# Fewer, wider weight transfers and an undivided filter band at the start of a convolution and maxout kernel

## The chip, the core and the metric

The kernel runs on one core of a Trainium2 chip. The metric is the device time of one execution in microseconds (us), as the median of several runs. One core has five engines with instruction streams of their own: TensorE (PE, with its weight loads shown as PEld), VectorE (DVE), ScalarE (ACT), GpSimd (POOL) and SyncE (SP), which issues nearly all transfers. Each engine takes its instructions in the order in which the program lists them, and waits for what they need.

## The reference

The input `x` is 8 sequences of 4160 tokens with 192 channels. First comes a causal convolution over 7 tokens whose weights are the softmax of a small table; the 192 channels are 8 heads of 24, and a head shares its 7 weights. Then a maxout layer with three weight matrices and an output matrix:

```python
w = softmax(weight, axis=-1)                       # 8 heads x 7 taps
out[b, s, head, c] = sum_k w[head, k] * x_pad[b, s + k, head, c]
x = out.reshape(33280, 192)
h = maximum(maximum(x @ w1, x @ w2), x @ w3)       # w1, w2, w3: 192 x 768
return h @ w_out                                   # w_out: 768 x 192
```

All of it is given and returned in 32-bit floats.

## The kernel before, in words

The 33280 tokens are 65 blocks of 512. The maximum is rewritten so that TensorE forms only two of the three products: with the differences `wd1 = w1 - w3` and `wd2 = w2 - w3`, the maximum of the three is `max(relu(y @ wd1), y @ wd2) + y @ w3`. The first part is `h`, in six column tiles `j` of 128. The rest, `y @ w3`, needs no maximum, so `w3 @ w_out` is worked out once (`m16`, by `make_m`) and is added in the output product. So the weights must land as 32-bit numbers, be subtracted (`make_wd`) and so be turned into the 16-bit `wd` before the first hidden tile can be formed.

**Steady state.** From block 2 on, each block has its hidden products (`l1`, line 521), per tile one relu on ACT (line 508) and one maximum on DVE (line 509), and the output products of the block before it (`st2`, line 585). TensorE's list is written out by hand in that order. It is without gaps from some 30 us on.

**Start.** All that the change touches lies in the first 20 us. The list of each engine there follows the order of the program text:

- Lines 241 to 245 issue, on SP: block 0's `x` (two transfers), block 1's `x` (one), then of `w3`, `w1`, `w2` the upper 128 rows in columns 0 to 255 (`load_wa`, lines 227 to 229, three transfers), the lower 64 rows of `w3` in all 768 columns (line 244, one), and the lower 64 rows of `w1` and `w2` in columns 0 to 255 (`load_wb`, lines 231 to 233, two). Behind the band's code, lines 303 to 306 issue the rest: `load_wa` for columns 256 to 511, `load_wb` for columns 256 to 767, `load_wa` for columns 512 to 767, then `w_out`, then blocks 2 and 3.
- The convolution is a product with a banded matrix `band` (128 rows, 8 heads, 134 columns). TensorE makes its 38 nonzero columns for 32 rows in two PSUM tiles (line 291, columns 0 to 27 and 28 to 37), and line 299 copies these to the four diagonal places `a` of 32 rows, ACT the wide part and DVE the narrow one, first for heads 5 to 7 and then for heads 0 to 4: 8 copies on each engine.
- `cast_dense(t, ...)` (lines 207 to 218) turns block t's `x` into 16 bits in two halves, `v` = 0 on DVE and `v` = 1 on POOL, in three column slots. For block 0 slots 1 and 2 come ahead of the band's copies and slot 0 between the two groups of heads.
- `conv_dense(t, copies, order)` (lines 384 to 401) is block t's convolution: two PSUM tiles `n`, 40 products each. `n` = 1 needs heads 5 to 7 alone, `n` = 0 needs heads 0 to 5. `copies[n]` is the engine that takes tile `n` out to `yd` (line 401).
- `copy_w3` (line 324, on ACT) copies `w3`'s lower 64 rows to the other half of the partitions, in 32 bits. `make_wd(n, j0, j1)` (line 320) makes the differences for tiles j0 to j1: `n` = 0 is `w1` upper, `n` = 1 is `w2` upper, `n` = 2 holds the lower rows of both and needs `copy_w3` for its columns.
- `l1_dense` (line 544) forms hidden tiles of blocks 0 and 1 in two parts: "F" with the upper rows (`n` = 0 and 1) and "H" with the lower ones (`n` = 2). `tops` gives for each tile one relu on ACT and one maximum on DVE (lines 508 and 509).
- `cross_wd`, `cast_w3`, `transpose_w3`, `make_m`, `first_hidden` and the casts of blocks 2 and 3 follow, and need all weights.

In what follows, "the relus 0 and 1" are those of block 0, tiles 0 and 1; then come block 1's for the same tiles, a 1.47 us fill with zeros (`zero_x(6)`, line 140, on ACT), and the relus of tiles 2 and 3.

Of the kernel before, what the change touches and what calls it, by code (L numbers as in the profile page):

```python
# [15 lines left out]
P = 128  # L16
KW = 7
PAD = KW - 1
NHEAD = 8
# [5 lines left out]
WIN = 32 + PAD  # L25
# [3 lines left out]
def kernel(  # L29
# [12 lines left out]
    nc = tc.nc  # L42
# [3 lines left out]
    H, KWs = weight.shape  # L46
    assert H == NHEAD and KWs == KW and D == GRP * NHEAD
    DFF = moe_w1.shape[1]
# [9 lines left out]
    for b in range(B):  # L58
        s = nfull * NBLK
        while s < SEQ:  # L60
            n = min(SEQ - s, NBLK - off)
# [57 lines left out]
    xin, xbuf, XBUF, loaded = {}, [], 7, set()  # L119
# [82 lines left out]
    NC, NSLOT, CYC = D // HALF, D // 32, 96  # L202
# [1 line left out]
    xz = {t: [const.tile([P, NQ, D], FP16, name=f"xz_{t}_{v}") for v in range(2)] for t in range(2)}  # L204
    xz[2], xz[3] = xz[0], xz[1]

    def cast_dense(t, copies, slots_=range(CYC // 32), keep=False):
        xf, _, parts = xin[t] if keep else xin.pop(t)
        for v, copy in enumerate(copies):
            if copy is None:  # L210
                continue
            for s in slots_:
                cut = GRP * (32 * s // GRP + 1)
                a, b = (32 * s, cut) if v == 0 else (cut, 32 * s + 32)
                for (rl, q0, q1) in parts:
                    copy(  # L216
                        out=xz[t][v][0:rl, q0:q1, :].rearrange("p q (k c) -> p q k c", c=CYC)[:, :, :, a:b],
                        in_=xf[0:rl, q0:q1, :].rearrange("p q (k c) -> p q k c", c=CYC)[:, :, :, a:b])
# [6 lines left out]
    PW = 2 * P  # L225

    def load_wa(f):
        for st, n, wsrc in ((w3s, 0, moe_w3), (ws, 0, moe_w1), (ws, 1, moe_w2)):
            nc.sync.dma_start(out=st[:, n, f], in_=wsrc[0:P, f])  # L229

    def load_wb(f):
        for st, lo, n, wsrc in ((ws, 0, 2, moe_w1), (ws, HALF, 2, moe_w2)):
            nc.sync.dma_start(out=st[lo:lo + HALF, n, f], in_=wsrc[P:D, f])
# [22 lines left out]
    def keep_warm(widths, pool, tag):  # L256

        ps = pool.tile([P, NBLK], FP32, tag=tag, name="idle")
        for n in widths:
            nc.tensor.matmul(ps[:, 0:n], lhsT=idle[:, 0:P], rhs=idle[:, 0:n], start=True, stop=True)  # L260
# [15 lines left out]
    band = bands[:, 0:NHEAD * BAND_W].rearrange("p (h w) -> p h w", w=BAND_W)  # L276
# [4 lines left out]
    nc.vector.reciprocal(out=wrec[:], in_=wrec[:])  # L281
    zero_x(4)
    nc.vector.tensor_scalar_mul(out=line[0:NHEAD, 31:31 + KW], in0=wexp[:, 0:KW], scalar1=wrec[:])
    cast_dense(0, (nc.vector.tensor_copy, nc.gpsimd.tensor_copy), (1, 2), keep=True)
    CUT = 28
    bands_ = []
    for lo, hi, copy in ((0, CUT, nc.scalar.copy), (CUT, WIN, nc.vector.tensor_copy)):
        bps = psq.tile([32, hi - lo + 3, NHEAD], FP32, tag="q", name=f"band_{lo}")
# [4 lines left out]
                             rhs=ident16[:, 0:4 * NHEAD], start=True, stop=True)  # L293
        bands_.append((lo, hi, copy, bps))
    keep_warm((NBLK, NBLK, P), psp, "p")
    for h0, h1 in ((5, NHEAD), (0, 5)):
        for lo, hi, copy, bps in bands_:
            for a in range(4):
                copy(out=band[32 * a:32 * a + 32, h0:h1, 32 * a + lo:32 * a + hi],
                     in_=bps[:, 0:hi - lo, h0:h1].rearrange("p c h -> p h c"))  # L300
        if h0:
            cast_dense(0, (nc.vector.tensor_copy, nc.gpsimd.tensor_copy), (0,))
    load_wa(slice(PW, 2 * PW))
    load_wb(slice(PW, DFF))
    load_wa(slice(2 * PW, DFF))
    nc.sync.dma_start(out=wos[:], in_=moe_w_out.rearrange("(j p) c -> p j c", p=P))
    load_x(2)
    load_x(3)
# [9 lines left out]
    def make_wd(n, j0, j1, eng=nc.vector):  # L318
        f = slice(P * j0, P * j1)
        eng.tensor_sub(out=wd[:, n, f], in0=ws[:, n, f], in1=w3s[:, n // 2, f])  # L320

    def copy_w3(copy, j0, j1):
        f = slice(P * j0, P * j1)
        copy(out=w3s[HALF:P, 1, f], in_=w3s[0:HALF, 1, f])  # L324
# [12 lines left out]
    def w_of(i, c, j):  # L337
        n = side(i, c)
        n = i if n == 0 else NC if n == 1 else 2
        return wd[HALF * i:HALF * (i + 1), n, P * j:P * (j + 1)]  # L340
# [43 lines left out]
    def conv_dense(t, copies, pools=((None, None),) * 2, order=(0, 1)):  # L384


        yd = dense[t] = ydp.tile([P, NC, NBLK], FP16, tag="yd", name=f"yd_{t}")
        for n in order:
            slots_ = ((0, 1, 2, 3), (4, 5, 4, 5))[n]
            pool, tag = pools[n]  # L390
            ps = (pool or psw).tile([P, NBLK], FP32, tag=tag or "w", name=f"D{n}_{t}")
            for (q, b, row_lo, rlen, lo, hi, cc) in chunks_of[t]:
                for v in range(2):
                    for g, s in enumerate(slots_):
                        h = (32 * s + 31 * v) // GRP
                        nc.tensor.matmul(  # L396
                            ps[32 * g:32 * g + 32, lo:hi],
                            lhsT=xz[t][v][0:rlen, q, 32 * s:32 * s + 32],
                            rhs=band[0:rlen, h, cc:cc + hi - lo],
                            start=(v == 0), stop=(v == 1), tile_position=(0, 32 * g))  # L400
            copies[n](out=yd[:, 2 * n, :], in_=ps[:])
# [49 lines left out]
    def y_all(t, i, c):  # L451
        if t < NDENSE:
            return dense[t][HALF * i:HALF * (i + 1), side(i, c), :]
        a = y_row(t, i)
        s0, s1, s2, s3 = (spot(t, i, c, r) for r in range(4))
        assert s3 - s2 == s1 - s0
        return bass.AP(tensor=a.tensor, offset=a.offset + P * s0,
                       ap=[list(a.ap[0]), [P * (s2 - s0), 2], [P * (s1 - s0), 2], [1, P]])
# [39 lines left out]
    def meet():  # L498

        emit(True)  # L500
        assert not ops
        clock[0] = clock[1] = 0

    def top(t, j, ps):
        if t not in hs:
            hs[t] = hp.tile([P, NJ, NBLK], FP16, tag="h", name=f"h_{t}")
        r = rp.tile([P, NBLK], FP16, tag="r", name=f"r_{t}_{j}")
        nc.scalar.activation(out=r[:], in_=ps[0][:], func=AF.Relu)  # L508
        nc.vector.tensor_max(out=hs[t][:, j, :], in0=r[:], in1=ps[1][:])  # L509
        done[t] = j + 1  # L510
# [20 lines left out]
    def l1_dense(tiles, parts="FH"):  # L531

        meet()
        for n, part in enumerate(parts):
            for t, j, pools in tiles:
                for i, (pool, tag) in enumerate(pools):
                    if (t, j, i) not in open_ps:
                        open_ps[t, j, i] = pool.tile([P, NBLK], FP32, tag=tag, name=f"l{tag}{i}_{t}_{j}")
                        begun.discard((t, j, i))
                    if part == "F":  # L540
                        a, b = wd[:, i, P * j:P * (j + 1)], dense[t][:, 0, :]
                    else:
                        a, b = w_of(i, NC - 1, j), y_all(t, i, NC - 1)
                    nc.tensor.matmul(open_ps[t, j, i][:], lhsT=a, rhs=b,  # L544
                                     start=(t, j, i) not in begun, stop=(t, j, i) in begun)
                    begun.add((t, j, i))

    def tops(*tiles):
        for t, j in tiles:
            top(t, j, (open_ps[t, j, 0], open_ps[t, j, 1]))  # L550
# [139 lines left out]
    PQ = ((psp, "p"), (psq, "q"))  # L690
    WW = ((psw, "w"), (psw, "w"))
    WPWQ = ((psw, "w"), (psp, "p"), (psw, "w"), (psq, "q"))
    ACT, DVE = nc.scalar.copy, nc.vector.tensor_copy
    GP = nc.gpsimd.tensor_copy
    conv_dense(0, (ACT, ACT), order=(1, 0))
    cast_dense(1, (DVE, GP), (1, 2, 0))
    zero_x(5, eng=nc.gpsimd)
    make_wd(0, 0, 2)
    make_wd(1, 0, 2)
    copy_w3(ACT, 0, 2)  # L700
    make_wd(2, 0, 2)
    conv_dense(1, (DVE, ACT), order=(1, 0))
    copy_w3(ACT, 2, 6)
    for n in range(NC):
        make_wd(n, 2, 4, nc.gpsimd)
    for n in range(NC):
        make_wd(n, 4, 6, nc.gpsimd)
    cast_w3(0, 6)
    GP(out=wo[:], in_=wos[:])
    l1_dense([(0, 0, PQ), (0, 1, PQ)], "F")  # L710
    l1_dense([(0, 0, PQ), (0, 1, PQ)], "H")
    tops((0, 0), (0, 1))
    l1_dense([(1, 0, WW), (1, 1, WW)], "HF")
    tops((1, 0), (1, 1))
    zero_x(6)
# [135 lines left out]
```

## Time and profile before

| | before |
|---|---|
| median of 3 runs | 453.19 us (453.03 to 454.11) |
| profiled execution, its own time | 454.16 us |
| its span, first to last instruction | 452.4 us |
| TensorE busy | 445.5 us, 98% of the span |
| mean granted TensorE clock | 1.000 of full speed |
| first gapless hidden products of block 2 (line 521) begin | 24.4 us |
| transfers of `w1`, `w2`, `w3` | 14 issues of 64 to 192 KB, by lines 229, 233 and 244 |

Times in the profile's rows are in us from the start of the span. A row of the timeline has start, duration, engine, line, operation, output and inputs, and how many instructions it merges; in brackets stands how long the engine had been idle and what released it. With `x2` the duration is that of both together. The chain of work that ended last is followed back from the last instruction. A row of the windows has, for one stretch, its length, the busy time of PE, PEld, DVE, ACT and POOL, the clock granted to TensorE, the busy share of the 16 DMA engines and the GB/s.

### The profile page before, as it was taken

What the parts mean: (1) busy time and instruction counts of PE and PEld (TensorE: products, weight loads), DVE (VectorE), ACT (ScalarE), POOL (GpSimd) and SP (SyncE); (2) the same over time, 40 slices, a digit from 0 to 9 for tenths busy, and PEclk for the clock granted to TensorE, in tenths of its full rate; (3) what the DMA queues carried; (4) which work ended last, traced back from release to release, by engine and by line L of the source; (5) the groups of instructions that cost most, each with busy time, mean ns of one, the idle gap of its engine ahead of it and who ended that gap; (6) DMA issues with size and microseconds to landing.
All of it is one profiled execution on the core that took longest, in us unless ns stands there. A gap on an engine that the chain in (4) does not pass through costs nothing.

```text
span 452.4 us, 18264 instructions
## 1 busy us (share of the span) xinstructions
PE 445.5 (98%) x7576; PEld 409.8 (91%) x7576; DVE 354.6 (78%) x607; ACT 320.2 (71%) x601; POOL 207.6 (46%) x239
## 2 busy tenths in 40 slices
PE   7999999999999999999999999999999999999997
PEld 4469999999999989999999999999999999999996
DVE  6668787878878787787887787887887887887775
ACT  6967767767777677676676776777776776776664
POOL 5864836556463533724824635525533644224000
PEclk9999999999999999999999999999999999999999
DMA  7968987696885659649649748657649668152123
GB/s 197 239 181 167 203 186 197 155 217 171 170 220 147 165 137 205 162 121 199 167 127 198 178 110 191 191 114 193 178 112 197 172 157 143 54 136 75 58 71 106
DMA packets 128163, 72.01 MB, mean 159 GB/s; under 512 B 52305, under 2 KB 127888, under 8 KB 128080
## 3 DMA queue, kind: packets, MB, share of 16 engines
q1 hardware_dynamic: 127919, 70.75, 65.9%
q8 instruction: 59, 0.97, 0.9%
q14 instruction: 25, 0.20, 0.2%
q10 hardware_dynamic: 160, 0.10, 0.1%
HBM read 33.28 MB, written 25.56 MB: 130 GB/s over the span
## 4 chain that ended last, share of the span: by engine, by line
PE 96%; DMA 1%; ACT 1%; SPq 1%; issue 1%; DVE 0%; ACTq 0%
PE po L585 36%; PE lq L521 32%; PE lp L521 22%; PE G L375 3%; DMA wall<-in_moe_w_dram 1%; ACT r L508 1%; PE D L396 1%; PE po L643 0%; PE po L616 0%; PE lw L544 0%; SPq L229 0%; SPq L167 0%; PE pm L355 0%; ACT wall L324 0%; PE lq L544 0%
## 5 line engine op out<-in xcount | busy, mean ns | idle before, releaser
L585 PE MATMUL po<-wo,h 64*128 64x192 f16 x3024 | 331.7, 243 | 0.0
L509 DVE TENSOR_TENSOR h<-r,lq 128x512 f16<-128x512 f16 x384 | 263.0, 686 | 86.2 <-ACT r L508 76.3
L508 ACT ACTIVATE r<-lp 128x512 f16<-128x512 f32 x384 | 228.9, 597 | 113.8 <-PE lp L521 103.0
L521 PE MATMUL lp<-yp,wd 64*128 64x512 f16 x1098 | 295.6, 376 | 0.0
L521 PE MATMUL lq<-yp,wd 64*128 64x512 f16 x1098 | 295.5, 376 | 0.0
L585 PEld LDWEIGHTS <-h 64*128 64x128 f16 x3024 | 242.7, 94 | 5.4 <-issue 4.1
L521 PEld LDWEIGHTS <-wd 64*128 64x128 f16 x2268 | 181.7, 94 | 14.8 <-issue 0.2
L199 POOL CAST x<-xf 103x768 f16<-103x768 f32 x122 | 97.3, 825 | 114.4 <-DMA xf<-in_x_dram 99.6
L585 PE MATMUL po<-m,yp 64*128 64x192 f16 x720 | 140.3, 243 | 0.0
L438 POOL COPY yp<-yp 64x1536 f16<-64x1536 f16 (+1 forms) x70 | 90.9, 1298 | 86.0 <-DMA yp<-ys 49.1
L593 DVE TENSOR_TENSOR o<-a,po 128x384 f32<-128x384 f32 x126 | 69.0, 547 | 0.0
L585 PEld LDWEIGHTS <-yp 64*128 64x128 f16 x720 | 66.3, 94 | 0.1
L592 ACT COPY a<-po 128x384 f32<-128x384 f32 x126 | 59.6, 473 | 0.0
L415 ACT CAST ys<-G 128x480 f16<-128x480 f32 (+1 forms) x53 | 25.4, 530 | 9.5 <-PE G L375 9.2
L415 DVE CAST ys<-G 128x480 f16<-128x480 f32 (+1 forms) x53 | 30.1, 610 | 0.0
L375 PE MATMUL G<-x,band 39*32 39x240 f16 (+3 forms) x1024 | 16.5, 242 | 0.0
L375 PEld LDWEIGHTS <-band 39*32 39x32 f16 x1024 | 10.2, 92 | 4.6 <-issue 4.1
L521 PE MATMUL lq<-yd,wd 64*128 64x512 f16 x36 | 9.7, 376 | 0.0
L521 PE MATMUL lp<-yd,wd 64*128 64x512 f16 x36 | 9.7, 376 | 0.0
L544 PEld LDWEIGHTS <-wd 128*128 128x128 f16 (+1 forms) x48 | 3.0, 95 | 7.3 <-issue 1.7
L396 PEld LDWEIGHTS <-xz 112*32 112x32 f16 x320 | 4.1, 96 | 2.9 <-issue 1.4
L216 POOL CAST xz<-xf 112x160 f16<-112x160 f32 (+2 forms) x18 | 5.1, 328 | 3.2 <-DMA xf<-in_x_dram 3.0
(75 smaller groups left out, 100.0 us busy)
## 6 DMA issues: line engine op xcount, KB each, us to landing
xf<-in_x_dram SPq DMA_DIRECT2D x113, 234.0 KB
out_dram<-o SPq DMA_DIRECT2D x62, 384.0 KB
xf<-in_x_dram SPq DMA_DIRECT2D x7, 204.8 KB
wall<-in_moe_w_dram SPq DMA_DIRECT2D x11, 128.0 KB
xf<-in_x_dram SPq DMA_DIRECT2D x3, 420.0 KB
yp<-ys SPq DMA_TRANSPOSE x70
out_dram<-o SPq DMA_DIRECT2D x5, 192.0 KB
wos<-in_moe_w_out_dram SPq DMA_DIRECT2D x1, 576.0 KB
```

What stands on the lines that cost most here:

```text
L199: nc.gpsimd.tensor_copy(out=x16s[t0][0:K, :, :, u, r, :].rearrange("p h j c -> p j h c"), in_=xf[0:K, 4 * r:4 * r + 4, :].rearrange("p j ( ...
L216: copy(out=xz[t][v][0:rl, q0:q1, :].rearrange("p q (k c) -> p q k c", c=CYC)[:, :, :, a:b], in_=xf[0:rl, q0:q1, :].rearrange("p q (k c) -> ...
L375: nc.tensor.matmul(G[2 * (k // per) + i][TOK * j:TOK * (j + 1), k % per, :], lhsT=band[row, h, HALF * i + LAP:HALF * i + KR], rhs=x16s[t0] ...
L396: nc.tensor.matmul(ps[32 * g:32 * g + 32, lo:hi], lhsT=xz[t][v][0:rlen, q, 32 * s:32 * s + 32], rhs=band[0:rlen, h, cc:cc + hi - lo], star ...
L415: copy(out=slots[t][:, i % 2, :, :, GRP * h0:GRP * (h0 + per)].rearrange("p u r (h c) -> p h (u r) c", c=GRP), in_=G[i][:].rearrange("p h ...
L438: nc.gpsimd.tensor_copy(out=yp[HALF * i:HALF * (i + 1), 1, :, :, :, :].rearrange("p i u k n -> p (i u k n)"), in_=yp[HALF * (1 - i):HALF * ...
L508: nc.scalar.activation(out=r[:], in_=ps[0][:], func=AF.Relu)
L509: nc.vector.tensor_max(out=hs[t][:, j, :], in0=r[:], in1=ps[1][:])
L521: nc.tensor.matmul(ps[i][:], lhsT=w_of(i, c, j), rhs=y_all(t, i, c), start=(n == 0), stop=(n == NC - 1))
L585: nc.tensor.matmul(ps[b0, i][:, s % 2, :], lhsT=a, rhs=b, start=first, stop=last)
L592: nc.scalar.copy(out=a[:], in_=ps[s - 1, 0][:])
L593: nc.vector.tensor_add(out=outs[t][:, s - 1:s + 1, :], in0=a[:], in1=ps[s - 1, 1][:])
```

## The change

Four things are altered, all in the first part of the program:

1. The band is copied for all heads at once and for three of the four places; the fourth place is copied by POOL from the first (16-bit, from on-chip memory). Block 0's casts are no longer split around it, and block 0's convolution takes `n` = 0 first.
2. The upper rows of the weights come in two column pieces (256 and 512 columns) and no longer in three, so the second `load_wa` covers columns 256 to 767 and stands ahead of the second `load_wb`: three issues fewer. The transfer of `w3`'s lower 64 rows, whole already, is as before.
3. Block 1's convolution tile `n` = 0 is taken out by ACT and no longer by DVE.
4. `copy_w3` for tiles 2 to 5 stands behind the relus of tiles 0 and 1 in ACT's list. POOL's list of `make_wd` is in the same order as before, with the text around it moved.

```diff
-    def cast_dense(t, copies, slots_=range(CYC // 32), keep=False):
-        xf, _, parts = xin[t] if keep else xin.pop(t)
+    def cast_dense(t, copies, slots_=range(CYC // 32)):
+        xf, _, parts = xin.pop(t)
...
-    cast_dense(0, (nc.vector.tensor_copy, nc.gpsimd.tensor_copy), (1, 2), keep=True)
+    cast_dense(0, (nc.vector.tensor_copy, nc.gpsimd.tensor_copy))
...
-    for h0, h1 in ((5, NHEAD), (0, 5)):
-        for lo, hi, copy, bps in bands_:
-            for a in range(4):
-                copy(out=band[32 * a:32 * a + 32, h0:h1, 32 * a + lo:32 * a + hi],
-                     in_=bps[:, 0:hi - lo, h0:h1].rearrange("p c h -> p h c"))
-        if h0:
-            cast_dense(0, (nc.vector.tensor_copy, nc.gpsimd.tensor_copy), (0,))
-    load_wa(slice(PW, 2 * PW))
+    for lo, hi, copy, bps in bands_:
+        for a in range(3):
+            copy(out=band[32 * a:32 * a + 32, :, 32 * a + lo:32 * a + hi],
+                 in_=bps[:, 0:hi - lo, :].rearrange("p c h -> p h c"))
+    nc.gpsimd.tensor_copy(out=band[96:P, :, 96:96 + WIN], in_=band[0:32, :, 0:WIN])
+    load_wa(slice(PW, DFF))
     load_wb(slice(PW, DFF))
-    load_wa(slice(2 * PW, DFF))
...
-    conv_dense(0, (ACT, ACT), order=(1, 0))
+    conv_dense(0, (ACT, ACT))
...
-    conv_dense(1, (DVE, ACT), order=(1, 0))
+    conv_dense(1, (ACT, ACT), order=(1, 0))
+    make_wd(0, 2, 4, nc.gpsimd)
+    make_wd(1, 2, 4, nc.gpsimd)
+    l1_dense([(0, 0, PQ), (0, 1, PQ)], "F")
+    l1_dense([(0, 0, PQ), (0, 1, PQ)], "H")
+    tops((0, 0), (0, 1))
     copy_w3(ACT, 2, 6)
-    for n in range(NC):
-        make_wd(n, 2, 4, nc.gpsimd)
+    make_wd(2, 2, 4, nc.gpsimd)
     for n in range(NC):
         make_wd(n, 4, 6, nc.gpsimd)
     cast_w3(0, 6)
     GP(out=wo[:], in_=wos[:])
-    l1_dense([(0, 0, PQ), (0, 1, PQ)], "F")
-    l1_dense([(0, 0, PQ), (0, 1, PQ)], "H")
-    tops((0, 0), (0, 1))
     l1_dense([(1, 0, WW), (1, 1, WW)], "HF")
```

## The prediction

> **What bounds the kernel now.** I read the page first.
>
> ```profile
> PE 445.5 (98%) x7576; PEld 409.8 (91%) x7576; DVE 354.6 (78%) x607; ACT 320.2 (71%) x601; POOL 207.6 (46%) x239
> ```
>
> TensorE is the bound over the span, so the change, which takes no product away, can only move the time at which TensorE comes to its gapless work. I therefore read the chain that ended last for the first 30 us.
>
> ```profile
> 3.71 6.13 DMA wall<-in_moe_w_dram
> 9.86 0.40 ACT wall L324
> 10.29 0.58 ACT yd L401
> 10.90 0.62 ACT wall L324
> ...
> 15.12 0.61 ACT r L508
> 15.75 0.70 DVE h L509
> ...
> 16.49 0.38 PE lq L544
> ```
>
> The chain starts from a transfer (`w3`'s lower 64 rows, landing at 9.84), runs along ACT's own list to 15.73, crosses DVE and is on TensorE from 16.49 on. Up to 16.49 an instruction more on ACT is paid in full; behind it the chain stays on TensorE, with one hole of 0.84 us at 27.88 that no wait explains.
>
> Next the timelines of ACT, TensorE and POOL there. The reader should see that ACT has no bracket after 9.86, thus no idle time.
>
> ```profile
> 9.86 0.40 ACT L324 COPY wall<-wall 64x256 f32<-64x256 f32 x1 [1.79 <-DMA wall<-in_moe_w_dram]
> 10.29 0.58 ACT L401 CAST yd<-D 128x512 f16<-128x512 f32 x1
> 10.90 0.62 ACT L324 COPY wall<-wall 64x512 f32<-64x512 f32 x1
> 11.54 1.08 ACT L508 ACTIVATE r<-lp 128x512 f16<-128x512 f32 x2
> 12.51 1.09 ACT L508 ACTIVATE r<-lw 128x512 f16<-128x512 f32 x2
> 13.63 1.47 ACT L140 CAST xf<-idle 32x1536 f32<-32x1536 f16 x1
> 15.12 1.09 ACT L508 ACTIVATE r<-lp 128x512 f16<-128x512 f32 x2
> ```
>
> ```profile
> 11.06 0.39 PE L544 MATMUL lp<-yd,wd 64*128 64x512 f16 x1 [1.08 <-DVE wd L320]
> ```
>
> ```profile
> 10.92 1.41 POOL L320 TENSOR_TENSOR wd<-wall 128x256 f16<-128x256 f32 x2 [1.34 <-DMA wall<-in_moe_w_dram]
> 12.66 0.73 POOL L320 TENSOR_TENSOR wd<-wall 128x256 f16<-128x256 f32 x1 [0.33 <-ACT r L508]
> 13.71 0.72 POOL L320 TENSOR_TENSOR wd<-wall 128x256 f16<-128x256 f32 x1 [0.33 <-DMA wall<-in_moe_w_dram]
> 15.47 1.42 POOL L320 TENSOR_TENSOR wd<-wall 128x256 f16<-128x256 f32 x2 [1.03 <-DMA wall<-in_moe_w_dram]
> ```
>
> POOL, which makes all differences from tile 2 on, waits for weights three times; the last piece lets it go at 15.47. Last, the DMA engines by stretch (the last two figures are share and GB/s):
>
> ```profile
> 6.00:9.30 3.30, 2.74 (x150) 2.12 (x138) 2.40 (x10) 1.87 (x5) 2.06 (x4) 1.00 1.02 232
> 9.30:10.20 0.90, 0.68 (x4) 0.10 (x1) 0.00 (x0) 0.34 (x1) 0.28 (x1) 1.00 0.33 80
> 10.20:14.20 4.00, 3.13 (x20) 1.22 (x22) 3.06 (x6) 3.90 (x8) 2.62 (x4) 1.00 0.74 217
> 14.20:16.00 1.80, 1.80 (x13) 0.51 (x7) 0.69 (x2) 1.77 (x3) 0.77 (x2) 1.00 1.05 341
> ```
>
> They run dry for 0.9 us at 9.3, because SP has not issued enough: the timeline has `load_wb`'s two issues from 8.17 to 10.04 and the last three `load_wa` ones only from 10.09.
>
> **The change part by part.**
>
> *Band and block 0.* ACT's copies of 84 and 140 elements take 217 and 264 ns: 0.84 ns an element, so 335 ns for 224. Three of them from 4.71 end at 5.8, where eight end at 6.73. DVE's 30 and 50 elements take 178 and 198 ns, so 230 ns for 80; three behind 4.98 end at 5.7. POOL's casts of block 0 end at 5.12; its copy of 32x304 waits for the two first places (5.1 and 5.2). No row has this copy: from below POOL's 240 ns-class rows (112x80 in 260 ns), from above its 64x512 copy of 609 ns; I take 0.45, as 304 elements lie between. It ends near 5.8, or 5.9 with the longer; behind it in POOL's list stands block 1's cast, which waits for its `x` until 7.18 anyway. The convolution of block 0 then runs as one piece from 5.9 to 7.2 (two of 0.64), where it ended at 7.42. That gains nothing: block 1's casts start at 7.15 when its `x` lands, its products end at 8.94 and the F products at 9.98, and the H products wait until 11.06, with 1.08 us to spare. If POOL's copy took 1 us more, this cover would still hold it.
>
> *ACT's list.* Between the landing at 9.84 and the relu of tile 2 ACT loses nothing and gains one evacuation, which DVE did at 10.92 (0.68 there, 0.58 on ACT). In front of relu 0 the new order is copy, evacuation, evacuation; the second evacuation takes the place of the 0.62 copy, so ACT is free at 11.5, and relu 0 starts at 11.54 as now, since its H products end then. Behind relu 1 the copy comes in with its spacing, 10.90 to 11.54: 0.64 us. Relus of block 1, the zero fill and relu 2 are later by that: 15.12 to 15.76. DVE has no slack to make it good (it idles 1.10 us for relu 2) and TensorE waits for DVE at 16.49. So **+0.64** on the path. DVE loses an evacuation in idle time: nothing.
>
> *Transfers already in flight.* `w3`'s lower rows and the lower rows of `w1`, `w2` for tiles 0 and 1 are issued before any altered transfer, but their tail now shares the DMA engines with wider pieces instead of having the dry stretch to itself. From below 0, because all ahead of them is unchanged. From above: the stretch from 9.30 to 10.58, when DVE gets the last, at 232 instead of 341 GB/s, 1.28 x 0.47 = 0.6. I take **+0.2**, nearer to the lower end, as most of their bytes have moved by 9.3.
>
> *Wider pieces.* The three upper pieces carry 768 KB, where POOL's first wait was for 384. The extra 393 thousand bytes at 217 to 341 GB/s are 1.15 to 1.8 us, so POOL starts its first two differences at 12.1 to 12.7 (now 10.92) and, as they are 0.7 each, ends them at 13.5 to 14.1. The lower pieces, 262 thousand bytes, follow 0.8 to 1.2 later: 12.9 to 13.9. From above, all of these bytes have landed by 15.47 in the trace of before. The third difference also needs the moved copy, which ends at 13.2 to 13.4. I take 13.9, by the 217 GB/s of the stretch in which they move; behind the second difference the third then ends at 14.8, the H products of tile 2 0.45 later (13.87 to their relu's earliest start now) at 15.25, and relu 2 (15.76, or 15.96 with the 0.2) finds them ready. So nothing on the path, with 0.7 us to spare. The three remaining differences wait for nothing further and end near 16.9, as now. SP: three issues of 0.43 to 0.58 fewer, and `w_out` and blocks 2 and 3 are issued 1.5 us earlier; POOL's use of them (18.23 and 19.56) lies beside TensorE's chain, so nothing.
>
> The Trainium skill's page "Perfetto Trace Analysis", section "DMA Optimizations", has rules for both sides: larger transfers use the memory better, yet splitting lets work start sooner where the DMA engines are idle. The rows above show both conditions, 1.02 busy and then 0.33. By the first rule alone POOL would be earlier and the sum would be ACT's 0.64, 453.8; by the second, the first wait grows by the time of the bytes added, and the sum is the one below.
>
> **Sum.** 0.64 + 0.2 = +0.84 us: the profiled execution's 454.16 (span 452.4 and 1.76 around it) would become 455.0. It stood 0.97 above the median of the runs, so from the median I forecast 453.19 + 0.84 = 454.0.
>
> **The rivals.**
>
> *Late lower pieces (slower).* POOL's third difference takes ACT's place on the path as soon as the lower pieces land later than 15.96 - 0.45 - 0.73 - 0.1 = 14.7; each us beyond costs one. For it: three waits of POOL for weights today, one of 1.03 us right there, and the lower rows now come last of all weights. Against: the dry 0.9 us at 9.3 will be filled. With the landing at the upper bound, 15.47: H products at 16.2, relu 2 at 16.65, +1.53, so 454.7; with one more us of stalled issue (`load_wb`'s first issue took 1.23 us where its second took 0.60) 455.7. It passes 0.3% from a landing of 15.3 on.
>
> *Covered.* The 0.84 us hole at 27.88 could close when transfers are earlier, or the copy could fit where ACT waits for late H products anyway. Then the sum is 0.84 - 0.84, 453.2. Against: the hole has no releaser in the trace, and ACT never idles between 9.86 and 15.7.
>
> *Faster.* If the filled dry stretch brought the first weights forward, each us at 9.84 would be a us at the end; 2.2 us would be needed to gain 1.4 on balance: 451.8. Against: these transfers are issued before the change begins to differ.
>
> **How the numbers follow.** What a measurement here tells from no change is about 0.3%, 1.36 us. Chances: the forecast 0.48 (its own range 453.6 to 454.6: 453.8 and 454.4 by the ends of the 0 to 0.6 term, and 0.2 for the scatter of medians), of which 0.02 passes the bound; late pieces 0.36, since a landing of 15.3 needs only 1.4 us over my value and the rows' spread is that wide; covered 0.10; faster 0.06. So slower 0.38, same 0.56, faster 0.06. The range drops the faster case and the far end of the late one: 453.1 to 455.7.
>
> **What would show it.** Right: ACT still without idle time from 9.86, the second copy of line 324 behind two relus, line 401 twice in a row near 10.3, relu 2 near 15.8 to 16.0; POOL's first row of line 320 near 12.5; a DMA share near 1 from 9.3 to 10.2; block 2's first product of line 521 at 25.2 instead of 24.4. Wrong: an ACT bracket before relu 2 that names TensorE, behind it a POOL row of line 320 that starts after 14.7; or TensorE stalled at block 0's convolution by POOL's copy past 8.

## The result and the profile after

The changed kernel takes 454.48 us in the median of 20 runs (453.63 to 455.65), the kernel before 453.61 us in as many on the same chips (452.90 to 454.94). The ratio is 1.0017, with a 95% interval of 1.0009 to 1.0025: **slower by 0.77 us (0.41 to 1.13)**; the two medians are 0.87 us apart. The forecast was +0.84; both lie inside the 0.3% (1.36 us) named there.

The two profiled executions can't be laid side by side by their ends: the one of before (454.16 us, span 452.4) has the hole of 0.84 us at 27.88, the one of after (453.63 us, span 451.8) has none. Where the change acts they can. After the change, the chain that ended last, in order of time (start, duration, what):

```profile
1.69 5.62 DMA xf<-in_x_dram
7.33 5.28 DMA wall<-in_moe_w_dram
...
12.77 1.42 POOL wd L317 x2
...
14.23 0.39 PE lq L541
...
24.72 0.37 PE lp L518
```

It no longer runs along ACT. It goes from a wide weight piece that lands at 12.61 over POOL's first two differences to TensorE, which has no gap from 14.23 to block 2's first product at 24.7. The F products of tiles 2 and 3 wait for POOL there, and the H products stand behind them:

```profile
13.55 0.39 PE L541 MATMUL lp<-yd,wd 128*128 128x512 f16 x1 [0.70 <-POOL wd L317]
14.23 0.39 PE L541 MATMUL lq<-yd,wd 128*128 128x512 f16 x1 [0.29 <-POOL wd L317]
...
15.01 0.39 PE L541 MATMUL lp<-yd,wd 64*128 64x512 f16 x1
```

(Line 317 is `make_wd`, 321 `copy_w3`, 398 the evacuation, 505 the relus, 541 `l1_dense`, 518 `l1`: the numbers of the changed kernel are three lower, and those of the experiments' kernels up to three lower.) ACT's timeline after the change:

```profile
9.51 0.40 ACT L321 COPY wall<-wall 64x256 f32<-64x256 f32 x1 [1.77 <-DMA wall<-in_moe_w_dram]
9.94 1.07 ACT L398 CAST yd<-D 128x512 f16<-128x512 f32 x2
11.08 1.08 ACT L505 ACTIVATE r<-lp 128x512 f16<-128x512 f32 x2
12.19 0.62 ACT L321 COPY wall<-wall 64x512 f32<-64x512 f32 x1
12.83 1.08 ACT L505 ACTIVATE r<-lw 128x512 f16<-128x512 f32 x2
13.94 1.47 ACT L140 CAST xf<-idle 32x1536 f32<-32x1536 f16 x1
15.44 1.08 ACT L505 ACTIVATE r<-lp 128x512 f16<-128x512 f32 x2
```

ACT is still without idle time from the first copy on, with the two evacuations in a row and the second copy behind two relus. Relu 2 comes 5.93 us behind the first copy (15.44 - 9.51) where it came 5.26 behind it (15.12 - 9.86): +0.67. So two paths end within some hundredths of each other: ACT is done with the fill at 15.41, and the H products of tile 2, behind POOL, end at 15.40. POOL and the DMA engines after the change (the window's last figures are share and GB/s):

```profile
5.38 0.44 POOL L300 COPY band<-band 32x304 f16<-32x304 f16 x1
...
12.77 4.24 POOL L317 TENSOR_TENSOR wd<-wall 128x256 f16<-128x256 f32 x6 [2.94 <-DMA wall<-in_moe_w_dram]
```

```profile
9.30:10.20 0.90, 0.90 (x4) 0.20 (x2) 0.03 (x1) 0.67 (x2) 0.53 (x1) 1.00 1.06 378
```

POOL waits once, for 2.94 us, where it waited three times in the first profile of before. That was one execution: in the two later profiles of before it waits once as well, but for 2.61 and 1.98 us, and starts at 11.68 and 11.81. The dry stretch of the DMA engines (share 0.33) is full (1.06); it too differs from one execution to the next, 0.33 to 0.89 in the ten profiles with three pieces against 0.99 to 1.06 in the four with wide ones. The six differences end at 17.0, where they ended at 16.9.

### The profile page after: what moved, and what is told of

Same layout as the page of the kernel before. It is cut to its first block, busy times and chain, and to the rows that moved or that the text cites. A ratio compares the mean times of both kernels' runs of the same rounds, so it can differ in the third digit from the quotient of the medians.

```text
span 451.8 us, 18253 instructions
## 1 busy us (share of the span) xinstructions
PE 445.3 (99%) x7576; PEld 409.2 (91%) x7576; DVE 353.1 (78%) x601; ACT 319.9 (71%) x597; POOL 208.2 (46%) x240
## 4 chain that ended last, share of the span: by engine, by line
PE 96%; DMA 2%; POOL 0%; SPq 0%; issue 0%; DVE 0%; POOLq 0%
PE po L582 36%; PE lq L518 32%; PE lp L518 22%; PE G L372 3%; DMA xf<-in_x_dram 1%; DMA wall<-in_moe_w_dram 1%; PE lw L541 1%; PE D L393 0%; PE po L640 0%; PE po L613 0%; PE lp L541 0%; POOL wd L317 0%; PE pm L352 0%; PE lq L541 0%; SPq L167 0%; PE pt L343 0%
## 5 line engine op out<-in xcount | busy, mean ns | idle before, releaser
L518 PEld LDWEIGHTS <-wd 64*128 64x128 f16 x2268 | 181.4, 94 | 14.7 <-issue 0.2
L372 PEld LDWEIGHTS <-band 39*32 39x32 f16 x1024 | 10.2, 91 | 4.6 <-issue 4.1
L216 POOL CAST xz<-xf 112x80 f16<-112x80 f32 (+2 forms) x18 | 5.2, 333 | 2.6 <-DMA xf<-in_x_dram 2.6
```

The costliest lines, as they stand in the source:

```text
L216: copy(out=xz[t][v][0:rl, q0:q1, :].rearrange("p q (k c) -> p q k c", c=CYC)[:, :, :, a:b], in_=xf[0:rl, q0:q1, :].rearrange("p q (k c) -> ...
L372: nc.tensor.matmul(G[2 * (k // per) + i][TOK * j:TOK * (j + 1), k % per, :], lhsT=band[row, h, HALF * i + LAP:HALF * i + KR], rhs=x16s[t0] ...
L518: nc.tensor.matmul(ps[i][:], lhsT=w_of(i, c, j), rhs=y_all(t, i, c), start=(n == 0), stop=(n == NC - 1))
```

## The experiments

Run times of this kernel scatter by 2 us from one execution to the next, so the intervals below reach half a microsecond and more each way, wide for parts of 0.6 us. ACT's first copy, which waits for a landing, itself starts at 8.95 to 10.10 in the 14 profiles taken. The experiments are therefore read inside each trace, **from ACT's first copy (line 324 of the kernel before) on**: to relu 2, which is ACT's path, and to block 2's first product, which is everything up to the gapless work. From there to TensorE's last product it is 423.75 us (423.74 to 423.81) in the 11 profiles without a hole behind it; the other three have 424.80 (the first of before), 425.00 (changed again) and 425.10 (fill on DVE).

| run | first copy | relu 2 behind it | block 2 behind it | ratio of times, 95% interval |
|---|---|---|---|---|
| before | 9.86 | 5.26 | 14.54 | |
| before again (first, second) | 8.95, 9.59 | 5.37, 5.27 | 14.65, 15.32 | |
| changed | 9.51 | 5.93 | 15.21 | 1.0017 (1.0009 to 1.0025) |
| changed again | 9.42 | 6.11 | 15.40 | |
| ACT's list alone | 9.53 | 5.93 | 15.21 | 1.0006 (0.9995 to 1.0018) |
| wide pieces alone | 9.37 | 6.04 | 15.31 | 1.0016 (1.0005 to 1.0027) |
| evacuation back on DVE | 9.28 | 5.87 | 15.16 | 1.0011 (0.9996 to 1.0026) |
| three pieces again | 9.67 | 5.93 | 15.21 | 1.0025 (1.0008 to 1.0042) |
| band alone | 10.10 | 5.27 | 14.55 | 1.0012 (0.9993 to 1.0031) |
| both undone | 9.79 | 5.93 | 15.21 | 1.0000 (0.9989 to 1.0010) |
| evacuation alone | 9.38 | 5.76 | 15.45 | 0.9995 (0.9982 to 1.0008) |
| fill on POOL | 9.02 | 5.11 | 14.40 | 0.9976 (0.9964 to 0.9989) |
| fill on DVE | 9.25 | 5.14 | 14.54 | 1.0006 (0.9993 to 1.0018) |

Each distance is read from one profiled execution, and the distances are not the whole time. One more difference stands at the end. From the end of TensorE's last product to the end of the span it is 2.93 to 2.94 us in the ten profiles with three pieces and 3.12 to 3.14 in the four with wide ones. Before and after:

```profile
447.30 2.14 PE L643 MATMUL po<-wo,h 128*128 128x192 f16 x24
```

```profile
446.57 2.14 PE L640 MATMUL po<-wo,h 128*128 128x192 f16 x24
```

The first ends at 449.44 in a span of 452.38, the second at 448.71 in one of 451.85. At its very end SP waits for five semaphores of transfers in a fixed order. With three pieces the last store has the fourth of them, with three issues fewer it has the first. In all 14 traces the wait for it ends 2.07 to 2.08 us behind the last product, and each wait that still follows takes 0.06 to 0.07 us: one with three pieces, four with wide ones. So the wide pieces cost **0.20 us** there. With the path this makes +0.67 + 0.20 = +0.87 us for the change and +0.77 + 0.20 = +0.97 for the wide pieces alone; the runs have +0.77 (0.41 to 1.13) and +0.73 (0.23 to 1.22).

In three experiments the runs do not follow the distance: both undone (+0.67 by the trace, 0.00 by the runs, -0.50 to +0.45), the evacuation alone (+0.50 to relu 2; -0.23, -0.82 to +0.36) and the fill on POOL (-0.14; -1.09, -1.63 to -0.50). What the executions without a profile gained elsewhere there is not shown. The distances below are therefore statements on the path of the profiled execution.

The theory: the instruction more on ACT is the cost. The rival: the wide pieces, late at POOL, are.

### Each part alone

```diff
# ACT's list alone, in the kernel before
-    conv_dense(1, (DVE, ACT), order=(1, 0))
+    conv_dense(1, (ACT, ACT), order=(1, 0))
...
+    l1_dense([(0, 0, PQ), (0, 1, PQ)], "F")
+    l1_dense([(0, 0, PQ), (0, 1, PQ)], "H")
+    tops((0, 0), (0, 1))
     copy_w3(ACT, 2, 6)
...
```

> The kernel before with ACT's list of the change alone: the evacuation of block 1's convolution tile 0 on ACT, and the copy of w3's lower rows for tiles 2 to 5 behind relus 0 and 1; three column pieces and the divided band stay. ACT theory (the evacuation added to ACT's list is the cost): +0.6 us over the kernel before, relu 2 some 5.9 us after the landing that ends ACT's idle time (5.26 in the kernel before), block 2's first hidden products at about 25.0. Piece theory (the wide upper pieces land late and hold POOL, then TensorE): 0, within 0.2.

```diff
# wide pieces alone, in the kernel before
-    load_wa(slice(PW, 2 * PW))
+    load_wa(slice(PW, DFF))
     load_wb(slice(PW, DFF))
-    load_wa(slice(2 * PW, DFF))
```

> The kernel before with the wide pieces alone (three transfers fewer). ACT theory: 0 to +0.2. Piece theory: POOL's first difference of tile 2 starts at 12.5 to 12.8, TensorE has no gap from the end of POOL's second one (about 14.2) on, block 2's first hidden products at 24.7, +0.6 to +0.9 us. If both paths are of nearly one length, +0.3 to +0.7 here and in the first experiment alike.

ACT's list alone gives the path of the whole change, 5.93 and 15.21, with no idle time on ACT between these rows:

```profile
9.53 0.40 ACT L324 COPY wall<-wall 64x256 f32<-64x256 f32 x1 [1.46 <-DMA wall<-in_moe_w_dram]
...
15.46 1.09 ACT L508 ACTIVATE r<-lp 128x512 f16<-128x512 f32 x2
```

The wide pieces alone give as much, 6.04 and 15.31, along the other path. The timelines of ACT and POOL with the wide pieces alone:

```profile
13.13 1.47 ACT L140 CAST xf<-idle 32x1536 f32<-32x1536 f16 x1
15.40 1.08 ACT L507 ACTIVATE r<-lp 128x512 f16<-128x512 f32 x2 [0.80 <-PE lq L543]
```

```profile
12.54 1.41 POOL L319 TENSOR_TENSOR wd<-wall 128x256 f16<-128x256 f32 x2 [2.92 <-DMA wall<-in_moe_w_dram]
14.20 2.78 POOL L319 TENSOR_TENSOR wd<-wall 128x256 f16<-128x256 f32 x4 [0.25 <-DMA wall<-in_moe_w_dram]
```

Here ACT, with its old list, was ready for relu 2 at 14.60 and idled 0.80 us for TensorE, whose H products waited for POOL's third difference (14.20 to 14.93), which a piece released that landed at 13.98. So neither theory alone holds: on the path each part costs 0.7 to 0.8 us by itself (15.21 and 15.31 against 14.54), and the two side by side cost no more than one. The runs put the wide pieces clear of 0; for ACT's list alone they have +0.27 us (-0.23 to +0.82), which leaves both 0 and 0.67 open.

### One part undone

```diff
# evacuation back on DVE, in the changed kernel
-    conv_dense(1, (ACT, ACT), order=(1, 0))
+    conv_dense(1, (DVE, ACT), order=(1, 0))
```

> The changed kernel with block 1's convolution tile 0 taken out by DVE again, so that ACT has no more work than in the kernel before; pieces wide. ACT theory: the cost goes, 0 to +0.2 us over the kernel before. Piece theory: it stays, +0.6 to +0.9. Both paths of one length: ACT gets idle time before relu 2, and +0.4 to +0.7 stays.

```diff
# three pieces again, in the changed kernel
-    load_wa(slice(PW, DFF))
+    load_wa(slice(PW, 2 * PW))
     load_wb(slice(PW, DFF))
+    load_wa(slice(2 * PW, DFF))
```

> The changed kernel with three column pieces again. ACT theory: the cost stays, +0.6 us over the kernel before. Piece theory: it goes, 0. The DMA share from 9.3 to 10.2 us falls back from 1.06 towards 0.33 under both, as SP again has too little issued by then.

Neither undoing gives the time back: 15.16 and 15.21 stay. With three pieces the share from 9.3 to 10.2 falls to 0.62 (not all the way to 0.33), and ACT's path keeps its 5.93. With the evacuation on DVE one reading was not expected:

```profile
9.28 0.40 ACT L321 COPY wall<-wall 64x256 f32<-64x256 f32 x1 [0.98 <-DMA wall<-in_moe_w_dram]
9.71 0.58 ACT L398 CAST yd<-D 128x512 f16<-128x512 f32 x1
10.80 1.08 ACT L505 ACTIVATE r<-lp 128x512 f16<-128x512 f32 x2 [0.50 <-PE lq L541]
11.90 0.62 ACT L321 COPY wall<-wall 64x512 f32<-64x512 f32 x1
```

The idle time is in front of relu 0, not of relu 2: ACT waits 0.50 us for the H products of tiles 0 and 1, and then pays the moved copy as before. With this landing the H products of tile 2 end at 14.93, 0.2 before ACT is ready for relu 2, so ACT's path is the longer one here. On ACT, then, it is not the evacuation that costs but the copy's place.

### Both undone, the band, and the evacuation by itself

The two diffs above at once, in the changed kernel, leave the band and the moved copy.

> The changed kernel with three pieces and with the evacuation back on DVE; what is left of the change is the band and the place of the copy of w3's rows. Two paths of nearly one length (each part alone costs 0.6 to 0.8, both together no more): only undoing both gives the time back, 0 within 0.2 us; relu 2 at 5.2 to 5.4 us behind the first row of the copy, block 2's first product 14.5 to 14.7 behind it (15.2 and more in the changed kernel and in each single undoing). If the moved copy or the band had a cost of its own, the 15.2 would stay.

```diff
# evacuation alone, in the kernel before
-    conv_dense(1, (DVE, ACT), order=(1, 0))
+    conv_dense(1, (ACT, ACT), order=(1, 0))
```

> The kernel before with one edit: block 1's convolution tile 0 is taken out by ACT. The copy of w3's rows stays in front of relu 0. If any one instruction of 0.5 to 0.6 us more ahead of relu 2 is paid (in front of relu 0 or behind it): relu 0 at 2.1 to 2.2 us behind the first row of the copy (1.68 in the kernel before), relu 2 at 5.7 to 5.9 (5.26), +0.5 to +0.6 us. If ACT has idle time in front of relu 0, as in the run with two parts undone: relu 0 and relu 2 unchanged, 0.

```diff
# band alone, in the kernel before
-    for h0, h1 in ((5, NHEAD), (0, 5)):
...
+        for a in range(3):
+            copy(out=band[32 * a:32 * a + 32, :, 32 * a + lo:32 * a + hi],
...
+    nc.gpsimd.tensor_copy(out=band[96:P, :, 96:96 + WIN], in_=band[0:32, :, 0:WIN])
...
+    conv_dense(0, (ACT, ACT))
```

> The kernel before with the band's part alone (undivided copies, POOL's copy of the fourth place, block 0's casts in one go, its convolution with tile 0 first). All theories: 0, within 0.2 us; block 0's convolution in one piece that ends near 7.2, relu 2 at 5.26 us behind the first row of line 324, as in the kernel before.

The first expectation failed: with both undone the 5.93 and 15.21 stay, and the band alone gives 5.27 and 14.55, which is the kernel before. So on the path the moved copy has the full cost by itself, though the runs of this kernel show none of it (0.00, -0.50 to +0.45). The evacuation alone has most of it: relu 0 at 2.16 behind the first copy instead of 1.68, relu 2 at 5.76, 0.50 later; its runs do not show that either. ACT's timelines of the two, both undone first:

```profile
10.22 0.59 ACT L399 CAST yd<-D 128x512 f16<-128x512 f32 x1
11.36 1.08 ACT L506 ACTIVATE r<-lp 128x512 f16<-128x512 f32 x2 [0.56 <-PE lq L542]
12.47 0.62 ACT L322 COPY wall<-wall 64x512 f32<-64x512 f32 x1
```

```profile
9.80 1.07 ACT L401 CAST yd<-D 128x512 f16<-128x512 f32 x2
10.90 0.62 ACT L324 COPY wall<-wall 64x512 f32<-64x512 f32 x1
11.54 1.09 ACT L508 ACTIVATE r<-lp 128x512 f16<-128x512 f32 x2
```

Between the landing and the H products of tiles 0 and 1 there is room on ACT for three instructions: where ACT waits for these products, relu 0 starts 1.52 and 1.57 us behind the first copy, and copy, evacuation, copy take 1.68. The kernel before has these three there. Put a fourth in and relu 0 is late by 0.5; take the second copy out and the room stands empty, while the copy costs 0.64 behind relu 1. The change fills the room with the evacuation, so its ACT part costs one instruction, not two.

### The ACT path shortened

```diff
# fill on POOL, in the kernel before
     zero_x(5, eng=nc.gpsimd)
+    zero_x(6, eng=nc.gpsimd)
...
-    zero_x(6)
```

> The kernel before with the zero fill ahead of relu 2 (line 140, 1.47 us on ACT) moved to POOL, behind its first fill, where POOL waits for weights until 10.92. ACT theory for the kernel before: relu 2 comes as soon as its H products end, 4.3 to 4.6 us behind the first row of the copy and not 5.26. TensorE then waits for POOL's difference for tiles 4 and 5, which the last piece holds, so block 2's first product gains 0.2 to 0.6 us: -0.2 to -0.6 us in all. If ACT were not the path in the kernel before: 0.

```diff
# fill on DVE, in the kernel before
     make_wd(1, 0, 2)
+    zero_x(6, eng=nc.vector)
...
-    zero_x(6)
```

> The kernel before with the zero fill ahead of relu 2 (line 140) on DVE, behind its first two differences, where it waits for weights for 1.57 us. POOL is not delayed now. Relu 2 comes as its H products end, 4.3 to 4.6 us behind the first row of the copy (5.11 with the fill on POOL), TensorE then waits for POOL's difference of tiles 4 and 5: block 2's first product at 14.1 to 14.4 behind the copy (14.40 with the fill on POOL, 14.54 in the kernel before); -0.2 to -0.9 us.

```profile
11.67 1.09 ACT L508 ACTIVATE r<-lw 128x512 f16<-128x512 f32 x2
14.13 1.08 ACT L508 ACTIVATE r<-lp 128x512 f16<-128x512 f32 x2 [1.37 <-PE lq L544]
```

With the fill on POOL (these two rows) ACT now waits 1.37 us for TensorE: the fill was on the path, and when 1.47 us are taken from it 0.15 us are gained before POOL's path takes over. Relu 2 came at 5.11, later than expected: POOL, done with both fills at 10.31, waited for weights until 11.50, 2.5 behind the first copy, which was 1.06 in the first profile of before and 2.73 in the second (there with relu 2 at 5.37). POOL's path is thus close behind ACT's in the kernel before as well. The times gained more than the path: 452.23 against 453.11 us, **0.9976 (0.9964 to 0.9989)**, faster than the kernel before. Its nine executions lie between 451.91 and 453.06, those of before between 452.51 and 454.92; what keeps the long ones away is not shown. On DVE the fill ends at 10.65 and holds up the third difference: it starts 1.43 behind the first copy where 0.6 to 0.74 is usual. Relu 0 comes 0.66 us later, relu 2 only 0.12 earlier, and block 2's first product no earlier (14.54).

### The two kernels again

> The changed kernel, once more, for its profile: relu 2 at 5.9 us behind the first row of the copy and block 2's first product at 15.2 (5.93 and 15.21 in its first profile), whatever the landing that ends ACT's idle time. POOL's first difference of tile 2 3.0 to 3.3 us behind the copy.

> The kernel before, once more, for its profile. If the 0.84 us hole of TensorE at 27.88 belongs to one execution and not to the kernel: no hole, 423.75 us from block 2's first product to the last one, as in the five later profiles (424.8 in the first one), a span near 451.3. If it belongs to the kernel: the hole is there again.

> The kernel before, a third profile: relu 2 at 5.26 to 5.4 us behind the first row of the copy and block 2's first product at 14.5 to 14.65. Whether the hole of TensorE comes again is open: one profile of two had it.

The hole does not come in every execution: two of three profiles of before are without it, and the first repeat has a span of 450.5. The fill on DVE has one of 0.36 us at the same place, with 15 products of block 3's convolution left, and one of 0.47 us at 32.73. What makes them is not shown. The second repeat shows another loss, of 0.7 us, in its chain:

```profile
12.04 8.88 DMA xf<-in_x_dram
...
21.07 1.66 POOL xz L216 x6
22.73 0.04 issue
22.78 1.04 PE D L396 x65
```

Block 2's `x`, which is issued behind all weights, landed at 20.9; POOL's casts came late and TensorE waited for them before block 2's convolution. The run with the evacuation alone shows the same (landing 20.8), hence a part of its 15.45. None of the four profiles with wide pieces shows it: there POOL's casts of blocks 2 and 3 follow its other work without waiting. The repeat of the changed kernel has relu 2 at 6.11, 0.2 later than expected, with ACT idle 0.23 us for TensorE: in that execution POOL's path was the longer one.

## Why the prediction was right, point by point

- **The sum and its sign**: +0.84 forecast, +0.77 (0.41 to 1.13) measured. That it came so near is in part luck. The forecast is 0.64 on ACT and 0.2 for transfers in flight; the traces have 0.67 up to block 2 and 0.20 at the end of the kernel, for a reason that the forecast did not have. And the wide pieces, put at nothing, would have cost as much as ACT's list; they add nothing on the path only because the two paths run side by side.
- **The signs**: ACT without idle time, the second copy behind two relus, two evacuations in a row, POOL's late start and the full DMA stretch are all there. The times named from the start of the span (relu 2 at 15.8 to 16.0, block 2 at 25.2) are not (15.44, 24.7), since ACT's first copy came at 9.51 where the forecast had 10.06 (9.86 + 0.2).
- **ACT's list, +0.64**: 0.67 in the traces of the changed kernel and of ACT's list alone. Right in size and in place: the evacuation in front takes the copy's place, the copy behind relu 1 is the price. That a removed evacuation would give nothing back follows from it, which the first expectations missed.
- **Transfers already in flight, +0.2**: not found. ACT's first copy comes at 9.28 to 9.51 with wide pieces and at 8.95 to 10.10 with three; DVE's third difference at 9.89 to 10.17 against 9.69 to 10.70. The lower bound, 0, was the value to take.
- **Wider pieces, nothing on the path with 0.7 us to spare**: the term that was mis-sized. POOL's start (11.94 to 12.77 in the four profiles with wide pieces against 12.1 to 12.7) and the landing of the lower pieces (13.98 with wide pieces alone against 13.9) were nearly as worked out, but the spare was about 0 after the change, and -0.2 in its repeat. Most of it, 0.55 us, went because the sum tied both paths to one landing: ACT's first copy came at 9.51 and not at 10.06, so ACT was ready for relu 2 at 15.41 and not at 15.96, while POOL's pieces came no earlier. The rest, 0.15, is that the H products ended at 15.40 and not at 15.25: left out was that they stand behind F products in TensorE's list, and that these waited for POOL's second difference until 14.2; from there TensorE's own list fills the time to block 2. The rival "late lower pieces" is thus the other half of the truth, though not by its condition, a landing after 14.7: with the landing at 13.98 the pieces alone put 0.77 on the path. Both rules that the prediction sets against each other show: the dry stretch was filled, and POOL's first wait grew (its start was at 10.92 to 11.94 in the ten profiles with three pieces).
- **Three issues fewer, nothing**: wrong. They moved the last store to another semaphore, and SP's waits at the end took 0.20 us longer in all four profiles with wide pieces.
- **Earlier issues, nothing**: wrong in some executions. Block 2's `x` is issued at 9.8 to 10.8 us with wide pieces and at 11.4 to 12.4 with three. With three pieces block 2's `x` came too late in two of ten profiles and cost 0.4 and 0.7 us (15.45 where 5.76 for relu 2 makes 15.04; 15.32 where 14.6 is usual), with wide pieces it never did in four. How much of the medians' difference it takes back was not measured.
- **Band, nothing**: right. POOL's copy took 0.44 (0.45 forecast), block 0's convolution ran from 5.93 to 7.0, and the band alone left the path as it was.
- **The hole**: no releaser shows for it, as the prediction read it, but the rival wrongly treated it as a property of the kernel that transfers might close.

## What to carry to other kernels

Count the room between two waits on the engine that the chain runs along, in instructions: one put in or moved behind the gate costs about its length on the path (0.50 and 0.67 here), one taken out may leave the room empty and give nothing back. A spare between two paths holds only as long as both start from the same event; here one path's landing came 0.55 us earlier than assumed, and most of the 0.7 was gone. When two changes touch two paths of nearly one length, neither "one alone" nor "one undone" shows the sum; the idle bracket of the engine where the paths meet says which of them was last. Where executions scatter by more than the effect, the distance between two rows of each trace shows the path. It is not the run time: the end of the span held 0.20 us of its own here, and in three experiments the runs did not follow the distance.

## What was not expected of the hardware

The repeat of the changed kernel was the slowest execution profiled, 455.01 us. Its DVE and POOL timelines:

```profile
24.50 1.53 DVE L404 COPY yd<-yd 64x512 f16<-64x512 f16 x1
```

```profile
22.74 3.15 POOL L199 CAST x<-xf 103x768 f16<-103x768 f32 x4
```

The 16-bit copy of line 404 (407 in the kernel before) takes 0.28 to 0.75 us in the other 13 profiles and took 1.53 here; it ended at 26.03, just after POOL's four casts in a row (25.89). The other 13 have a pattern. In the three in which no POOL instruction was running when the copy started it took 0.29 us. In the other ten it ended 0.14 to 0.15 us after the POOL instruction that was then running. Here it ended 0.14 us after the one behind that. From block 2's first product to the last one this execution took 425.0 us instead of 423.75. The Trainium skill's page "SBUF — State Buffer", section "Who interferes with whom", says that VectorE's copies in a two-port mode and GpSimd contend for one pair of ports, that whoever issues first has it for the whole instruction while the other is blocked, and that the order of issue decides who blocks. The ten profiles agree with that, if the copy was the one blocked; in the repeat the copy lost to a second POOL instruction as well (0.83 us each). No run here varied it by itself, and no trace names the mode that the copy ran in.
